# Output tiles treated four at a time, third products accumulated on their own, small filter operations on GpSimd, and a new order

## The chip, the cores and the metric

The kernel runs on one core of a Trainium2 chip. That core has five engines that work at the same time: TensorE (PE) for matmuls, VectorE (DVE) and GpSimd (POOL) for elementwise work, ScalarE (ACT) for activations, scalings and copies out of the matmul accumulators (PSUM), and SyncE (SP), whose queue issues most transfers. GpSimd's queue issues the transfers that add what they carry to what lies at their destination. The metric is the device time of one execution in microseconds; lower is better.

## The reference

The input x has 2,048 steps of 640 channels. Two branches are computed from it and mixed by a gate of one number per step:

```
g = sigmoid(sum(x * gate_w))                       # one gate per step
a = x * (irfft(rfft(kv) * rfft(ssm_k)) + kv * D)   # kv = (k filtered by 4 taps) * v; one filter of 2,048 taps per channel
h = shift(gelu(layernorm(x) @ w1)) @ w2            # four channel groups shifted by +1, -1, +2, -2 steps
x1 = x + h
b = x1 + gelu(layernorm(x1) @ w3) @ w4
out = g * a + (1 - g) * b
```

The four shifts of the hidden layer and the causal filter of 2,048 taps per channel are what make it more than a chain of matmuls.

## The kernel before

**The filter branch.** The 640 channels are five chunks of 128. The 2,048 steps are four blocks of 512. Each block is transformed by matmuls with the matrices of a folded real Fourier transform (`h_chunk` for the filter, `x_fwd` for kv); before that, `h_fold`, `h_even`, `kv` and `kv2` fold the data by its symmetries on DVE. The result of a chunk lies in `HF` (filter) and `XF` (signal): four blocks, a real and an imaginary part, 512 values. `unit(c)` then forms, for a chunk c, each output block o as the sum over a <= o of filter block a times signal block o - a. It treats output blocks in pairs: blocks 2 and 3 first, then 0 and 1. A complex product is made of three real ones: two in one instruction (into places 0 and 1 of an accumulator) and a third from the sum of real and imaginary part (place 2). For a > 0 the products go to a second buffer `TT`, and all three are added to the accumulator `ACC` in one instruction of DVE, or by one accumulating transfer of GpSimd's queue. Two subtractions and additions then write the block's real and imaginary part over `XF`.

**The end.** `final(g, o, q, k)` makes two tiles of 128 steps of output block o: tile 4o + q and its mirror 4o + 3 - q, for channel group g (g = 0 is chunks 0 to 2, 384 channels; g = 1 is chunks 3 and 4, 256 channels). PE computes the even and the odd half of the inverse transform, ACT copies them out, DVE forms their sum (first tile) and difference, PE turns the difference upside down with a flip matmul, ACT scales it by the gate, DVE multiplies by x. For g = 0 an accumulating transfer adds the pair to the output; for g = 1 DVE adds the other branch, which lies in `X`, and SP stores the result. There are 16 such calls. `base` and `mm4` write the other branch of the first 384 columns to the output: a store and an accumulating transfer for each tile. An accumulating transfer of `final` comes after those of the same tiles.

**The order.** Every instruction is recorded as an operation with what it reads and writes. `SEQUENCE` is a list of all 1,171 operations, written out; each engine and queue takes its own in that order and waits, by semaphores, for those of other engines that it depends on. `PLACES` puts the matmul results into PSUM banks. `ON` is a string of digits: wherever the program has a choice (`turn`: scale on ACT or DVE, copy by DVE or by transfer, add by DVE or by transfer), a 1 takes the other one than the default. `schedule` also keeps large transposing transfers and large accumulating transfers apart: each kind waits for the ones of the other kind that stand ahead of it in the list.

**GpSimd before.** Its queue has 44 operations: 15 small powers for the layer norms (`pool_pow`), 5 accumulating transfers of `unit`, 16 of `mm4` and 8 of `final`.

Of the kernel before, what the change touches and what calls it, by code (L numbers as in the profile page):

```python
# [446 lines left out]
def bass_gated_mix__ssm_conv_h3__mixer_s_mlp__prompt_kernel(  # L447
# [34 lines left out]
    def ps(n, cls):  # L482
# [3 lines left out]
    SEQUENCE = [1, 4, 5, 6, 26, 7, 3, 45, 24, 8, 0, 49, 50, 51, 55, 48, 68, 9, 10, 11, 12, 13, 14, 15, 16, 69, 17,  # L486
# [59 lines left out]
    PLACES = [4, 1, 7, 6, 5, 4, 6, 1, 1, 7, 0, 6, 3, 0, 2, 1, 3, 2, 3, 6, 7, 2, 1, 2, 7, 3, 5, 0, 3, 6, 4, 1, 1, 6,  # L546
# [622 lines left out]
```

## Time and profile before

| | us |
|---|---|
| median of 3 runs (221.81 to 223.04) | 221.84 |
| the profiled execution | 222.27 |
| its span, first to last instruction | 220.2 |
| VectorE busy | 212.1 |
| TensorE busy | 209.0 |
| ScalarE busy | 196.5 |
| GpSimd busy | 45.7 |

The span is what the trace covers; the profiled execution took 2.07 us more than that. Nearly all elementwise work of DVE is recorded under line 660 (`tt`), ACT's under line 670 (`act`), the matmuls under line 692 (`mm`), and transfers under line 237, because helpers record them. A group of instructions is therefore told apart by its shape. Records of consecutive instructions overlap a little, and ends of matmuls are modelled, so that busy time and count times mean differ.

### The profile page before, as it was taken

How to read it: one execution, taken by the hardware profiler on the slowest of the kernel's cores; microseconds unless marked ns; L12 is line 12 of the kernel's file. 1: busy time of each engine (PE TensorE's matmuls, PEld its weight loads, DVE VectorE, ACT ScalarE, POOL GpSimd, SP SyncE). 2: the span in 40 equal slices, each digit the busy share in tenths (PEclk: the TensorE clock that was granted, in tenths of full speed). 3: DMA queues.
4: the chain of work that ended last, by engine and by line, in shares of the span. 5: the costliest groups of instructions: out<-in, count | busy, mean ns of one | idle time of the engine just before them, and what ended most of it. 6: DMA issues, size and time to landing. Idle time of an engine off the chain costs nothing.

```text
span 220.2 us, 3837 instructions
## 1 busy us (share of the span) xinstructions
PE 209.0 (95%) x1401; PEld 125.7 (57%) x1410; DVE 212.1 (96%) x418; ACT 196.5 (89%) x326; POOL 45.7 (21%) x48
## 2 busy tenths in 40 slices
PE   6899999999999999999999999999999999999961
PEld 2598755554664446665446565456665445776730
DVE  5999999999999999999999999999999998999993
ACT  2499999999999999999999999999798978558981
POOL 1331102400010001001380103331101060645440
PEclk9999999999999999999999999999999999999995
DMA  6999998999979995898486893793198299366696
GB/s 170 346 233 214 246 207 231 177 236 193 284 246 204 383 198 95 162 174 185 120 147 110 201 193 43 163 174 71 19 160 182 65 219 246 39 74 71 74 179 119
DMA packets 79440, 37.73 MB, mean 171 GB/s; under 512 B 59001, under 2 KB 76990, under 8 KB 79422
## 3 DMA queue, kind: packets, MB, share of 16 engines
q1 hardware_dynamic: 73920, 31.91, 63.3%
q0 software_dynamic: 5328, 5.51, 18.9%
q8 instruction: 11, 0.18, 0.3%
q10 hardware_dynamic: 174, 0.07, 0.2%
q14 instruction: 7, 0.06, 0.1%
HBM read 14.88 MB, written 5.77 MB: 94 GB/s over the span
## 4 chain that ended last, share of the span: by engine, by line
DVE 57%; PE 28%; DMA 5%; ACT 5%; issue 3%; SPq 0%
DVE arena L660 46%; PE PSall L692 28%; ACT arena L670 5%; DVE arena L665 4%; DMA arena<-arena 3%; DVE arena L861 3%; DVE arena L980 2%; DMA arena<-in_A_q_dram 2%; DVE arena L946 1%; DVE arena L862 0%; DVE arena L866 0%; SPq L237 0%; DVE arena L735 0%; DVE arena L704 0%
## 5 line engine op out<-in xcount | busy, mean ns | idle before, releaser
L692 PE MATMUL PSall<-arena 128*128 128x512 bf16 (+5 forms) x1340 | 201.7, 309 | 3.4 <-ACT arena L670 1.3
L660 DVE TENSOR_TENSOR arena<-arena 128x1024 bf16<-128x1024 bf16 (+14 forms) x270 | 175.1, 712 | 1.7 <-DMA arena<-arena 0.9
L692 PEld LDWEIGHTS PSall<-arena 128*128 128x128 bf16 x1349 | 121.6, 98 | 82.7 <-ACT arena L670 3.3
L670 ACT ACTIVATE arena<-PSall 128x512 bf16<-128x512 f32 (+7 forms) x157 | 94.1, 659 | 9.6 <-PE PSall L750 4.9
L670 ACT ACTIVATE arena<-arena 128x640 bf16<-128x640 bf16 (+5 forms) x107 | 93.5, 904 | 1.9 <-DVE arena L660 1.8
L237 POOL DMA_DIRECT2D out_dram<-arena x24 | 24.1, 1133 | 67.7 <-ACT arena L670 51.7
L869 POOL TENSOR_TENSOR arena<-arena 128x2 f32<-128x2 f32 (+2 forms) x15 | 17.3, 1157 | 58.0 <-DVE arena L866 42.3
L670 ACT ACTIVATE arena<-PSall,arena 128x640 bf16<-128x640 f32 (+2 forms) x32 | 20.5, 652 | 6.8 <-PE PSall L692 6.6
L237 POOL DMA_DIRECT2D arena<-arena x5 | 4.9, 978 | 43.2 <-DVE arena L660 43.2
L980 DVE SCALAR_TENSOR_TENSOR arena<-PSall,arena 128x640 bf16<-128x640 f32 x16 | 12.9, 816 | 0.3
L665 DVE TENSOR_SCALAR arena<-arena 128x640 bf16<-128x640 bf16 (+6 forms) x35 | 11.9, 358 | 0.1
L861 DVE BATCH_NORM_STATS2 arena<-arena 128x6 f32<-128x320 bf16 x20 | 9.0, 484 | 1.3 <-DMA arena<-in_A_q_dram 1.3
L715 PE MATMUL PSall<-arena 128*128 128x512 bf16 x15 | 5.4, 529 | 2.2 <-DVE arena L712 2.2
L670 ACT ACTIVATION_READ_ACCUMULATOR arena<-arena 128x1 f32 x28 | 5.7, 204 | 0.0
L946 DVE TENSOR_SCALAR arena<-arena 32x256 bf16<-32x256 bf16 (+1 forms) x22 | 5.3, 240 | 0.4
L715 PEld LDWEIGHTS PSall<-arena 128*128 128x128 bf16 x15 | 1.8, 128 | 5.0 <-issue 2.5
L922 PE MATMUL PSall<-arena 128*128 128x128 bf16 x40 | 3.4, 220 | 0.9 <-DVE arena L665 0.9
L922 PEld LDWEIGHTS PSall<-arena 128*128 128x128 bf16 x40 | 2.4, 97 | 1.3 <-DVE arena L665 1.3
L866 DVE SCALAR_TENSOR_TENSOR arena<-arena 128x2 f32<-128x2 f32 (+2 forms) x19 | 2.9, 155 | 0.0
L718 ACT ACT_TABLE_LOAD x1 | 1.3, 1283 | 1.3 <-PEq L1154 1.3
L862 DVE BATCH_NORM_AGGREGATE arena<-arena 128x2 f32<-128x12 f32 x10 | 1.7, 192 | 0.0
L980 DVE DVE_READ_ACCUMULATOR arena<-PSall,arena 128x1 f32 x16 | 1.3, 80 | 0.0
(19 smaller groups left out, 2.9 us busy)
## 6 DMA issues: line engine op xcount, KB each, us to landing
arena<-in_A_ssm_k_dram SPq DMA_DIRECT2D x5, 512.0 KB, 5.2
arena<-in_A_q_dram SPq DMA_DIRECT2D x6, 320.0 KB, 5.7
arena<-in_B_w_dram SPq DMA_DIRECT2D x1, 1920.0 KB, 8.4
out_dram<-arena SPq DMA_DIRECT2D x16, 96.0 KB, 3.9
arena<-arena POOLq DMA_DIRECT2D x4, 384.0 KB, 5.0
out_dram<-arena POOLq DMA_DIRECT2D x16, 96.0 KB, 3.6
arena<-in_A_q_dram SPq DMA_DIRECT2D x8, 192.0 KB, 4.1
out_dram<-arena POOLq DMA_DIRECT2D x8, 192.0 KB, 4.0
```

The costliest lines, as they stand in the source:

```text
L237: fn = lambda e: e.dma_start(out, in_, **kw)
L660: P.op(eng, lambda e: e.tensor_tensor(o, real(a), real(b), op), [a, b], [o], dve_ns(o, [a, b], 2) if eng == "dve" else 500)
L665: P.op(eng, lambda e: e.tensor_scalar(o, real(a), s1, s2, op0=op0, **({} if op1 is None else {"op1": op1})), [a] + aps, [o], dve_ns(o, [a] ...
L670: P.op("act", lambda e: e.activation(real(o), real(a), f, bias=bias, scale=scale, **({"accum_out": accum} if accum is not None else {})), ...
L692: fns.append(lambda e, l=l, r=r, i=i: e.matmul(real(o), l, r, start=(i == 0), stop=(i == last)))
L715: P.op("pe", lambda e: e.matmul(real(pw), warm[:, 0:128], warm[:, 128:640], start=True, stop=True), [warm], [pw], 427.0 if i < 14 else 216.0)
L861: P.op("dve", lambda e, o=o, i=i: e.bn_stats(o, i), [i], [o], 400)
L866: P.op("dve", lambda e: e.scalar_tensor_tensor(o, a, x, b, op0=op0, op1=op1), [a, b] + aps, [o], n_of(o) / 0.96 + 65)
L869: P.op("pool", lambda g: g.tensor_tensor(o, a, e, ALU.pow), [a, e], [o], dur)
L922: P.op("pe", [lambda e, c=c, pb=pb, xn=xn: e.transpose(real(pb)[:, 128 * c:128 * (c + 1)], xn[:, 128 * c:128 * (c + 1)], ident) for c in r ...
L946: P.op("dve", lambda e, o=hT[q, 4, c0:c0 + n], i=hx[q, :]: e.tensor_scalar(o, i, 1.0, None, op0=ALU.mult), [hx[q, :]], [hT[q, 4, c0:c0 + n ...
L980: P.op("dve", lambda e: e.scalar_tensor_tensor(x, real(pr), 1.0, x, op0=ALU.mult, op1=ALU.add, accum_out=st[1, 0][:, t:t + 1]), [pr, x], [ ...
```

## The change

- `unit` adds the third product by itself where o0 = 2 and a is 1 or 2: the first two are added in one step, the third in another, each by DVE or by transfer according to `ON`, with a transfer as the third's default. `ACC` and `TT` are laid out with the three places outermost. From chunk 2 on, the third product for a = 2 has a buffer of its own, `TB2`. Chunk 4 is treated in three steps (blocks 2 and 3, then 1, then 0).
- `final(g, o, k)` makes all four tiles of an output block: one load of x, one sum and one difference for both halves, one product and one store or accumulating transfer for four tiles in their natural order. Only the last block of g = 1 is still treated tile by tile. There are 8 calls. The buffers `gyA` are three of four tiles (five of two before), `abA` two (four before).
- Small operations of `h_fold` and `h_even` (columns of 1 and 4 values, rows of 512 values on one partition) go to GpSimd unless `ON` keeps them on DVE.
- The DVE copy in `mm1` that moves shifted groups names the column before its own as read.
- `SEQUENCE` (now 1,147 operations), `PLACES` and `ON` are new throughout. With the new `ON`, three of the 25 small operations stay on DVE. `unit` has ten accumulating transfers: eight of a third product, one of the first two products, one of a whole sum. GpSimd's queue has 67 operations.

```diff
-    SEQUENCE = [1, 4, 5, 6, 26, 7, 3, 45, 24, 8, 0, 49, 50, 51, 55, 48, 68, 9, 10, 11, 12, 13, 14, 15, 16, 69, 17,
...
+    SEQUENCE = [26, 1, 8, 5, 0, 4, 6, 25, 3, 9, 10, 11, 12, 27, 13, 14, 15, 16, 28, 46, 52, 45, 39, 53, 49, 50, 54,
...
-    ACC, TT = [V(oB + 3072 * i, 3072).rearrange("p (o m n) -> p o m n", o=2, m=3) for i in range(2)]
+    ACC, TT = [V(oB + 3072 * i, 3072).rearrange("p (m o n) -> p m o n", m=3, o=2) for i in range(2)]
+    TB2 = V(oHF + 4096, 1024).rearrange("p (o n) -> p o n", o=2)
...
+    quad = lambda o, n: V(o, 4 * n).rearrange("p (t d) -> p t d", t=4)
+    qA = [quad(o, 384) for o in (oHF + 8192, oHF + 9728, oHF + 5120, oHF + 6656)]
+    qB = [quad(oHF + 12288 + 1024 * k, 256) for k in range(4)]
+    abA = [quad(oW2 + 1536 * i, 384) for i in range(2)]
+    gyA = [quad(o, 384) for o in (oHF, oHF + 1536, oB + 12288)]
+    abB = [quad(oB + 8192 + 1024 * i, 256) for i in range(4)]
+    gyB = [quad(oHF + 16384 + 1024 * i, 256) for i in range(4)]
...
+    def small_tt(o, a, b, op):
+        tt(o, a, b, op, "dve" if turn(False) else "pool")
...
-        tt(k[:, 0, 0:1], k[:, 0, 0:1], Dcol[:, c:c + 1], ALU.add)
+        small_tt(k[:, 0, 0:1], k[:, 0, 0:1], Dcol[:, c:c + 1], ALU.add)
...
-            tt(fo[:, e, :, 128], k[:, :, 384], k[:, :, 128], op)
+            small_tt(fo[:, e, :, 128], k[:, :, 384], k[:, :, 128], op)
...
-        tt(o[0:1, 0, 0], ev[0:1, 1, :, 0], ev[0:1, 0, :, 0], ALU.add)
-        tt(o[0:1, 1, 0], ev[0:1, 1, :, 0], ev[0:1, 0, :, 0], ALU.subtract)
+        small_tt(o[0:1, 0, 0], ev[0:1, 1, :, 0], ev[0:1, 0, :, 0], ALU.add)
+        small_tt(o[0:1, 1, 0], ev[0:1, 1, :, 0], ev[0:1, 0, :, 0], ALU.subtract)
...
-                         [hx[q, :]], [hT[q, 4, c0:c0 + n]], n / 3.84 + 65)
+                         [hx[q, :], hT[q, 4, c0 - 1:c0]], [hT[q, 4, c0:c0 + n]], n / 3.84 + 65)
...
-    ADDS = ()
+    SPLIT = ((2, 1), (2, 2))
...
-        for o0 in (2, 0):
-            for a in range(o0 + 2):
+        for o0, o1 in ((2, 4), (0, 2)) if c < 4 else ((2, 4), (1, 2), (0, 1)):
+            for a in range(o1):
...
+                own = a == 2 and c >= 2
...
+                third = TB2[:, 0:n] if own else to[:, 2]
...
-                if turn((o0, a) in ADDS):
-                    P.dma("pool", acc, tmp, accum=True)
-                else:
-                    tt(acc, acc, tmp, ALU.add)
+                parts = [(acc[:, 0:2], tmp[:, 0:2], False), (acc[:, 2], third, True)] if (o0, a) in SPLIT else [(acc, tmp, False)]
+                for x, y, away in parts:
+                    if turn(away):
+                        P.dma("pool", x, y, accum=True)
+                    else:
+                        tt(x, x, y, ALU.add)
...
+    def final(g, o, k):
...
+        qt, gy, ab = (qA, qB)[g][k], (gyA[k % 3], gyB[k])[g], (abA[k % 2], abB[k])[g].rearrange("p (q e) d -> p q e d", q=2)
+        rows = lambda a, t, m: bass.AP(a.tensor, a.offset + 128 * (4 * o + t) * D + 128 * c0, [[D, 128], [128 * D, m], [1, n]])
+        P.dma(sp, qt, rows(A_q, 0, 4))
+        for q in range(2):
+            scale(qt[:, q], qt[:, q], gst[3][:, 4 * o + q:4 * o + q + 1], True)
+        last = g == 1 and o == 0
+        both = [slice(q, q + 1) for q in range(2)] if last else [slice(0, 2)]
+        for q in range(2):
+            pr = ps(2, "inv")[:, :, 0:n]
...
+            act(ab[:, q], pr, ACTF.Copy)
+        for h in both:
+            tt(gy[:, h], ab[:, h, 0], ab[:, h, 1], ALU.add)
+            tt(ab[:, h, 1], ab[:, h, 0], ab[:, h, 1], ALU.subtract)
+        for q in range(2):
+            pf = ps(1, "fl")[:, 0:n]
+            mm(pf, [(flip, ab[:, q, 1])])
+            act(gy[:, 3 - q], pf, ACTF.Copy, scale=gst[3][:, 4 * o + 3 - q:4 * o + 4 - q])
+        for h in [slice(t, t + 1) for t in (0, 3, 1, 2)] if last else [slice(0, 4)]:
             tt(gy[:, h], gy[:, h], qt[:, h], ALU.mult)
+            if g:
+                tt(gy[:, h], gy[:, h], X[:, 4 * o + h.start:4 * o + h.stop, hs], ALU.add)
+                P.dma(sp, rows(out, h.start, h.stop - h.start), gy[:, h])
+            else:
+                P.dma("pool", rows(out, 0, 4), gy, accum=True)
...
         for o in (3, 2, 1, 0):
-            for q in range(2):
-                at(final, g, o, q, 2 * (3 - o) + q)
+            at(final, g, o, 3 - o)
```

More of the change, by code (lines that the diff above doesn't have):

```diff
@@ L484, in ps @@
         return v if n == 1 else v.rearrange("p (b n) -> p b n", b=2)
-    SEQUENCE = [1, 4, 5, 6, 26, 7, 3, 45, 24, 8, 0, 49, 50, 51, 55, 48, 68, 9, 10, 11, 12, 13, 14, 15, 16, 69, 17,
[59 rows of a table removed]
-    PLACES = [4, 1, 7, 6, 5, 4, 6, 1, 1, 7, 0, 6, 3, 0, 2, 1, 3, 2, 3, 6, 7, 2, 1, 2, 7, 3, 5, 0, 3, 6, 4, 1, 1, 6,
[6 rows of a table removed]
-    ON = ("0000000011111111011011111111111100010000010000101111000000000000001000010010000100000100000100000000"
-          "0000000000000000000000000000000")
+    SEQUENCE = [26, 1, 8, 5, 0, 4, 6, 25, 3, 9, 10, 11, 12, 27, 13, 14, 15, 16, 28, 46, 52, 45, 39, 53, 49, 50, 54,
[57 rows of a table added]
+    PLACES = [6, 3, 4, 7, 4, 6, 2, 4, 7, 3, 4, 3, 0, 1, 6, 0, 1, 2, 0, 2, 6, 1, 1, 7, 5, 4, 5, 1, 2, 7, 3, 2, 7, 6,
[6 rows of a table added]
+    ON = ("0000000011111111111111111111000000111000000011101000000000000000001011110000100000000100000100100000"
+          "1010000010000100100000000000000100000001001000000000000000000000000")
     HW = S + 4
@@ L613, in bass_gated_mix__ssm_conv_h3__mixer_s_mlp__prompt_kernel @@
     pair = lambda o, n: V(o, 2 * n).rearrange("p (t d) -> p t d", t=2)
-    qA = [pair(oHF + 8192 + 768 * k if k < 5 else oHF + 4096 + 768 * (k - 5), 384) for k in range(8)]
-    qB = [pair(oHF + 12288 + 512 * k, 256) for k in range(8)]
-    abA = [pair(oW2 + 768 * i, 384) for i in range(4)]
-    gyA = [pair(oHF + 768 * i, 384) for i in range(5)]
-    abB = [pair(oB + 8192 + 512 * i, 256) for i in range(8)]
-    gyB = [pair(oHF + 16384 + 512 * i, 256) for i in range(8)]
+    quad = lambda o, n: V(o, 4 * n).rearrange("p (t d) -> p t d", t=4)
[5 more added lines that the diff above has]
+    gyB = [quad(oHF + 16384 + 1024 * i, 256) for i in range(4)]
     sm = V32(oSm, 388)
@@ L862, in ln_bn, with stt @@
         P.op("dve", lambda e: e.bn_aggr(bna[:, t, :], bns[k]), [bns[k]], [bna[:, t, :]], 120)
-    def stt(o, a, x, b, op0, op1):
+    def stt(o, a, x, b, op0, op1, eng="dve"):
         aps = [x] if not isinstance(x, float) else []
-        P.op("dve", lambda e: e.scalar_tensor_tensor(o, a, x, b, op0=op0, op1=op1), [a, b] + aps, [o], n_of(o) / 0.96 + 65)
+        P.op(eng, lambda e: e.scalar_tensor_tensor(o, a, x, b, op0=op0, op1=op1), [a, b] + aps, [o], n_of(o) / 0.96 + 65)
     def pool_pow(o, a, e, dur=900):
@@ L1021, in unit @@
         tt(H4[:, :, 1], H4[:, :, 1], H4[:, :, 0], ALU.subtract)
-        for o0 in (2, 0):
-            for a in range(o0 + 2):
+        for o0, o1 in ((2, 4), (0, 2)) if c < 4 else ((2, 4), (1, 2), (0, 1)):
+            for a in range(o1):
                 lo = max(o0, a)
-                n, x0 = o0 + 2 - lo, lo - a
-                acc, tmp = ACC[:, lo - o0:2], TT[:, 0:n]
+                n, x0 = o1 - lo, lo - a
+                own = a == 2 and c >= 2
+                acc, tmp = ACC[:, :, lo - o0:o1 - o0], TT[:, :, 0:n]
                 to = tmp if a else acc
+                third = TB2[:, 0:n] if own else to[:, 2]
                 u, v = H4[:, a, 1], HD[:, a]
                 uv = bass.AP(u.tensor, u.offset, [u.ap[0], [0, n], [v.offset - u.offset, 2], [1, 512]])
-                tt(to[:, :, 0:2], X4[:, x0:x0 + n], uv, ALU.mult)
-                tt(to[:, :, 2], SX[:, x0:x0 + n], H4[:, a, 0].unsqueeze(1).to_broadcast([128, n, 512]), ALU.mult)
+                tt(to[:, 0:2].rearrange("p m o n -> p o m n"), X4[:, x0:x0 + n], uv, ALU.mult)
+                tt(third, SX[:, x0:x0 + n], H4[:, a, 0].unsqueeze(1).to_broadcast([128, n, 512]), ALU.mult)
                 if not a:
                     continue
-                if turn((o0, a) in ADDS):
-                    P.dma("pool", acc, tmp, accum=True)
-                else:
-                    tt(acc, acc, tmp, ALU.add)
-            Y = XF[:, c, o0:o0 + 2]
-            tt(Y[:, :, 0], ACC[:, :, 2], ACC[:, :, 1], ALU.subtract)
-            tt(Y[:, :, 1], ACC[:, :, 2], ACC[:, :, 0], ALU.add)
-            scale(Y[0:1, :, :, 0:128], ACC[0:1, :, 0:2, 0:128], 1.0, True)
-    def final(g, o, q, k):
+                parts = [(acc[:, 0:2], tmp[:, 0:2], False), (acc[:, 2], third, True)] if (o0, a) in SPLIT else [(acc, tmp, False)]
[4 more added lines that the diff above has]
+                        tt(x, x, y, ALU.add)
+            Y, R = XF[:, c, o0:o1], ACC[:, :, 0:o1 - o0]
+            tt(Y[:, :, 0], R[:, 2], R[:, 1], ALU.subtract)
+            tt(Y[:, :, 1], R[:, 2], R[:, 0], ALU.add)
+            scale(Y[0:1, :, :, 0:128].rearrange("p o r n -> p r o n"), R[0:1, 0:2, :, 0:128], 1.0, True)
+    def final(g, o, k):
         c0, c1 = GROUPS[g]
@@ L1046, in final @@
         hs = slice(128 * c0, 128 * c1)
-        ta, tb = 4 * o + q, 4 * o + 3 - q
-        qt, gy, ab = (qA, qB)[g][k], (gyA[k % 5], gyB[k])[g], (abA[k % 4], abB[k])[g]
-        two = lambda a: a[:, ta:tb + 1:tb - ta, hs]
-        rows = lambda a, lo, m: bass.AP(a.tensor, a.offset + 128 * ta * D + lo, [[D, 128], [128 * D * (tb - ta), 2], [1, m]])
-        P.dma(sp, qt, rows(A_q, 128 * c0, n))
-        scale(qt[:, 0], qt[:, 0], gst[3][:, ta:ta + 1], True)
-        pr = ps(2, "inv")[:, :, 0:n]
-        for e in range(2):
-            mm(pr[:, e].rearrange("p (c d) -> p c d", d=128), [(G[:, j, e ^ (j // 2), 128 * q:128 * (q + 1)], XF[:, c0:c1, o, e ^ (j // 2), 128 * j:128 * (j + 1)])
-                          for j in range(4)])
@@ L1057, in final @@
-        act(ab, pr, ACTF.Copy)
-        tt(gy[:, 0], ab[:, 0], ab[:, 1], ALU.add)
-        tt(ab[:, 1], ab[:, 0], ab[:, 1], ALU.subtract)
-        pf = ps(1, "fl")[:, 0:n]
-        mm(pf, [(flip, ab[:, 1])])
-        act(gy[:, 1], pf, ACTF.Copy, scale=gst[3][:, tb:tb + 1])
-        if not g:
-            tt(gy, gy, qt, ALU.mult)
-            P.dma("pool", rows(out, 0, n), gy, accum=True)
-            return
-        for h in (slice(0, 2),) if k < 6 else (slice(0, 1), slice(1, 2)):
-            tt(gy[:, h], gy[:, h], qt[:, h], ALU.mult)
-            tt(gy[:, h], gy[:, h], two(X)[:, h], ALU.add)
-            t = ta if h.start == 0 else tb
-            P.dma(sp, bass.AP(out.tensor, out.offset + 128 * t * D + 128 * c0, [[D, 128], [128 * D * (tb - ta), h.stop - h.start], [1, n]]), gy[:, h])
+        qt, gy, ab = (qA, qB)[g][k], (gyA[k % 3], gyB[k])[g], (abA[k % 2], abB[k])[g].rearrange("p (q e) d -> p q e d", q=2)
@@ new lines, in final @@
+        rows = lambda a, t, m: bass.AP(a.tensor, a.offset + 128 * (4 * o + t) * D + 128 * c0, [[D, 128], [128 * D, m], [1, n]])
[6 more added lines that the diff above has]
+            pr = ps(2, "inv")[:, :, 0:n]
+            for e in range(2):
+                mm(pr[:, e].rearrange("p (c d) -> p c d", d=128), [(G[:, j, e ^ (j // 2), 128 * q:128 * (q + 1)], XF[:, c0:c1, o, e ^ (j // 2), 128 * j:128 * (j + 1)])
+                              for j in range(4)])
+            act(ab[:, q], pr, ACTF.Copy)
```

128 rows, old and new, of tables (PLACES, SEQUENCE) are left out of this document.

## The prediction

> **What bounds the kernel now.** I read the totals first, then busy time by stretch, then the chain of waits, then the groups by shape. The first line is the engines' totals; the next three are stretches (start:end, then busy us of each engine, instruction counts in brackets).
>
> ```profile
> PE 209.0 (95%) x1401; PEld 125.7 (57%) x1410; DVE 212.1 (96%) x418; ACT 196.5 (89%) x326; POOL 45.7 (21%) x48
> 10.00:199.00 189.00, 188.10 (x1259) 112.91 (x1265) 186.77 (x335) 178.01 (x290) 36.10 (x34) 1.00 0.84 174
> 199.00:209.00 10.00, 9.59 (x75) 7.04 (x74) 9.93 (x26) 9.67 (x20) 4.50 (x4) 1.00 0.67 73
> 209.00:217.00 8.00, 4.30 (x28) 2.32 (x26) 7.84 (x29) 5.62 (x12) 2.38 (x2) 0.82 0.92 156
> ```
>
> From 10 to 199 us TensorE and VectorE are both full: 0.9 us of recorded idle on PE, 2.2 us on DVE. After 199 DVE stays full (17.77 of 18 us) and PE empties. So the run has a body in which two engines run abreast, and a tail of 18 us in which DVE is the bound. The chain and PE's timeline say the same (start us, length us, what):
>
> ```profile
> 176.97 6.79 DMA arena<-arena
> 205.95 4.19 DVE arena L660 x16
> 210.19 5.25 DVE arena L660 x18
> 216.66 0.29 DVE arena L660
> 213.31 0.28 PE L692 MATMUL PSall<-arena 128*128 128x256 bf16 x1 [1.16 <-ACT arena L670]
> 214.82 0.61 PE L692 MATMUL PSall<-arena 128*128 128x256 bf16 x2 [0.49 <-DVE arena L660]
> L692 PE MATMUL PSall<-arena 128*128 128x512 bf16 x48 | 10.5, 379 | 0.0
> ```
>
> DVE ends at 216.95 us and the span at 220.2, so 3.25 us follow it. One accumulating transfer (176.97) holds DVE up. The last row is PE between 100 and 110 us: 48 matmuls of 512 columns in 10 us, one each 0.21 us, with no idle time. The change leaves the matmuls as they are. Hence what it takes from DVE in the body can bring PE's stream forward only by what PE loses there now.
>
> **DVE's work, recounted.** Durations by shape (count | busy us of the group, mean ns of one):
>
> ```profile
> L660 DVE TENSOR_TENSOR arena<-arena 128x1024 bf16<-128x1024 bf16 (+14 forms) x270 | 175.1, 712 | 1.7 <-DMA arena<-arena 0.9
> L660 DVE TENSOR_TENSOR arena<-arena 128x3072 bf16<-128x3072 bf16 x9 | 15.7, 1749 | 0.1
> L660 DVE TENSOR_TENSOR arena<-arena 128x2048 bf16<-128x2048 bf16 x40 | 48.1, 1214 | 0.1
> L660 DVE TENSOR_TENSOR arena<-arena 128x1536 bf16<-128x1536 bf16 x16 | 15.1, 947 | 0.2 <-ACT arena L670 0.2
> L660 DVE TENSOR_TENSOR arena<-arena 128x1024 bf16<-128x1024 bf16 x80 | 52.0, 682 | 1.0 <-DMA arena<-arena 0.9
> L660 DVE TENSOR_TENSOR arena<-arena 128x768 bf16<-128x768 bf16 x8 | 4.4, 550 | 0.0
> L660 DVE TENSOR_TENSOR arena<-arena 128x512 bf16<-128x512 bf16 x22 | 9.0, 417 | 0.1
> L660 DVE TENSOR_TENSOR arena<-arena 128x384 bf16<-128x384 bf16 x16 | 5.4, 348 | 0.0
> L660 DVE TENSOR_TENSOR arena<-arena 128x256 bf16<-128x256 bf16 x24 | 6.1, 283 | 0.1
> L660 DVE TENSOR_TENSOR arena<-arena 1x512 bf16<-1x512 bf16 x10 | 4.1, 408 | 0.0
> L660 DVE TENSOR_TENSOR arena<-arena 128x4 bf16<-128x4 bf16 x10 | 1.6, 166 | 0.0
> L665 DVE TENSOR_SCALAR arena<-arena 128x2048 bf16<-128x2048 bf16 x4 | 2.9, 733 | 0.0
> L665 DVE TENSOR_SCALAR arena<-arena 128x640 bf16<-128x640 bf16 x16 | 6.6, 430 | 0.0
> ```
>
> By the first row 270 instructions of 0.712 us (192.2) keep DVE busy for 175.1 us, so each runs 0.063 us into the next, and an instruction saved is worth its duration less 0.063.
>
> - Small filter operations. The choices (the n-th digit of ON flips the n-th choice) send 22 to GpSimd: ten of 1x512, nine of 128x4, three of 128x1 (taken as 0.15). 4.08 + 1.49 + 0.45 - 22 x 0.063 = 4.6 us off DVE.
> - Adds in unit. Before, 9 of 3,072 and 6 of 1,536 elements; after, 9 of 2,048, 2 of 1,024 and 9 of 1,536, the rest going by ten transfers instead of five: 21.4 - 20.8 + 5 x 0.063 = 0.9 us off. That is little: the thirds leave, but transfers that carried whole adds come back.
> - Finals. Before: 16 each of 384 and 256, 8 of 768, 12 of 512, 8 of 256, in all 21.8 us in 60 instructions. After: 8 of 768, 6 of 512, 4 of 256, 4 of 1,536, 6 of 1,024, 8 of 256, in all 18.2 us in 36. 3.6 - 24 x 0.063 = 2.1 us off.
> - Unit 4 in three steps instead of two: four instructions more, 0.4 us on.
> - Choices that swap DVE and ACT: a tap of 2,048 and a normalisation of 640 come to DVE (0.73, 0.43), with six short copies (an estimate of 0.25 each, below the 0.43 of 640 elements), and one near 0.4 leaves: 2.25 less seven overlaps, 1.8 us on.
>
> Sum: 4.6 + 0.9 + 2.1 - 0.4 - 1.8 = 5.4 us off DVE, of 212.1. At most 2.1 of it lies in the tail.
>
> **What it is worth in the body.** PE's columns do not change, so I take only the 0.9 us that PE idles there by record; the bounds are 3 us sooner, were more of PE's loss hidden in the modelled ends, and 2 us later, if the new order stalls it somewhere. Two new costs lie here.
>
> First, accumulating transfers.
>
> ```profile
> arena<-arena POOLq DMA_DIRECT2D x4, 384.0 KB, 5.0
> arena<-arena POOLq DMA_DIRECT2D x1, 768.0 KB, 6.5
> out_dram<-arena POOLq DMA_DIRECT2D x16, 96.0 KB, 3.6
> out_dram<-arena POOLq DMA_DIRECT2D x8, 192.0 KB, 4.0
> out_dram<-arena SPq DMA_DIRECT2D x4, 64.0 KB, 2.0
> out_dram<-arena SPq DMA_DIRECT2D x6, 128.0 KB, 2.5
> ```
>
> Eight of the new ten carry 256 KB, so about 4.5 us each. I added up DVE's work from each product to the first instruction that needs the sum or overwrites the source. Unit 0's transfer has 6.3 us and unit 1's last one 5.1; in units 3 and 4 two follow one another, with 10.4 us for the pair, just enough. If one lands like that of 176.97 (6.79 us) DVE waits some 2 us. DVE's 5.4 us of relief covers that, so I cost it at nothing; without that cover it is 2 to 4 us. Behind a waiting transfer the GpSimd queue holds the small operations and normalisation powers that follow it; their readers on PE come some 8 us of PE work later.
>
> Second, GpSimd beside DVE.
>
> ```profile
> L869 POOL TENSOR_TENSOR arena<-arena x15: 560/858/3991, 4.5 to 142.6; 128x2 f32<-128x2 f32 x8, 128x1 f32<-128x1 f32 x4, 128x4 f32<-128x4 f32 x3
> 109.89 3.99 POOL L869 TENSOR_TENSOR arena<-arena 128x4 f32<-128x4 f32 x1
> 109.44 5.02 DVE L660 TENSOR_TENSOR arena<-arena 128x1024 bf16<-128x1024 bf16 x6
> ```
>
> One GpSimd power took 3.99 us beside six DVE instructions that ran their normal time (two of 1,024, three of about 2,048 and one of 1x512: 5.4 less five overlaps of 0.063 is 5.1; 5.02 measured). So GpSimd waited and DVE did not. But those powers read four numbers at most, and the new ones read 512. I take no cost to DVE, by that row; the bounds are 0 and 10 x 1.16 us (the 15 powers' 17.3 us over 15, if each instruction shut DVE out for its whole length).
> [...]
>
> **Start and tail.**
>
> ```profile
> 3.09 1.04 SPq L237 DMA_DIRECT2D arena<-in_B_w_dram  x2
> 9.08 0.82 PE L692 MATMUL PSall<-arena 128*128 128x128 bf16 x15
> 200.74 0.91 POOL L237 DMA_DIRECT2D out_dram<-arena  x1 [1.78 <-ACT arena L670]
> L670 ACT ACTIVATE arena<-PSall 128x768 bf16<-128x768 f32 x3 | 2.4, 792 | 0.1
> L670 ACT ACTIVATE arena<-PSall 128x512 bf16<-128x512 f32 x8 | 4.7, 588 | 0.1
> L670 ACT ACTIVATE arena<-PSall,arena 128x384 bf16<-128x384 f32 x4 | 2.3, 578 | 0.4 <-PE PSall L692 0.4
> L670 ACT ACTIVATE arena<-PSall,arena 128x256 bf16<-128x256 f32 x8 | 3.7, 473 | 1.0 <-PE PSall L692 1.0
> ```
>
> The last four rows are ACT's after 199.2 us. PE's first real matmul is at 9.08 us, and needs half of w1. The half that is used first is now issued one place sooner on SP (two issues take 1.04 us, so 0.5 us sooner), but the first tile is normalised behind more statistics. I take 0.3 us sooner, from 0 to 0.5.
>
> The last MLP tile has left ACT when its transfer is issued, at 200.74. From there the new order gives ACT one inverse of 768, four of 512 and two of 768, three flips of 384 and four of 256, two scalings and two short row copies (the last four at an estimated 0.45) before the inverses of final g = 0, o = 0 are all evicted: 2.4 + 2.4 + 1.7 + 1.9 + 1.8, less 1.0 for overlaps like DVE's, is 9.2 us, so about 209.7. That final's buffer is also gyA[0], which final g = 0, o = 3 used: its 384 KB transfer waits for the MLP tile's (3.6 us, 204.3) and takes about 5, to 209.3. Both say 209 to 209.7; I take 209.2. DVE then has 20 instructions: two of 768, twelve of 256, three of 1,024, one of 1,536 and two of 512, 8.3 less 20 x 0.063 = 7.1 us, to 216.3 where it was 216.95. But the last store is now 256 KB instead of 64: by the rows of 64 and 128 KB (0.5 us per 64 KB) 1.5 more, by those of 384 and 768 KB 0.75; I take 0.9. Tail: -0.65 + 0.9 = +0.25, from -1.5 to +1.5. So most of what DVE saves at the end goes into coarser steps.
>
> The profiled execution took 222.27 us, 2.07 over its span and 0.43 over the median. Its change is -0.3 - 0.9 + 0.25 = -0.95; taken off the median, 221.84, that is 220.9.
>
> **Rivals.** About 1% is what can be told from no change here.
> - As worked out: 220.9, its own range 219.6 to 222.5. For it: PE full in the body. Chance 0.45 with the rest of the cases within 1%.
> - The relief reaches PE: the new order has no stall in the body (-3.0), and tail and start give -0.3 between them: 218.5, its own range 217.3 to 219.6. For it: 5.4 us of slack that DVE never had, and ACT 11 us short of full in the body. Against it: 0.9 us of recorded idle. Chance 0.30.
> - GpSimd shuts DVE out: each of the ten 1x512 operations stops DVE for 0.56 us (the shortest power) to 1.16. That is 5.6 to 11.6 us against 5.4 saved, and the tail's +0.25: 222.3 to 228.3, about 225.3. It eats the saving from 0.54 us each, and passes 1% slower from about 0.75 each. For it: the 3.99 us show the two engines do meet at something. Against it: no DVE instruction was stretched. Chance 0.20.
> - The accumulation does not leave DVE: two of the ten thirds stay (units 0 and 2), and the waits on paired transfers come at 2 to 4 us uncovered: 224.5. Chance 0.05.
>
> Faster 0.30, same 0.45, slower 0.25. The range is 217.8 to 225.5: it leaves out the fastest quarter of the fast case (0.07) and the upper half of the third (0.10).
>
> **What would show it.** DVE busy near 206.7 with the 2,048 group at 1,214 ns: the recount holds. Any DVE group longer than before, or DVE idle released by nothing, next to GpSimd rows of 1x512: the third case. PE full from 10 to 199 with no earlier end: the body as worked out. DVE waiting at final g = 0, o = 0 near 209 on a GpSimd transfer or on ACT, and a last store of 3 us: the tail. A last matmul before 212 us would prove me wrong on the fast side.

## The result and the profile after

The changed kernel takes 236.27 us (median of 4 runs, 234.85 to 236.62) against 221.82 us before (median of 4): a ratio of 1.063, with a 95% interval from 1.057 to 1.068. It is 6% slower, outside my range and past its slow end. The profiled execution took 234.85 us, with a span of 233.1.

Totals of the changed kernel:

```profile
PE 211.6 (91%) x1401; PEld 125.2 (54%) x1410; DVE 216.8 (93%) x388; ACT 194.4 (83%) x323; POOL 77.0 (33%) x71
```

DVE has 30 instructions fewer than before and is busy 4.7 us longer. GpSimd has 23 more and is busy 31 us longer. Busy time by stretch of the changed kernel (start:end, length, then PE, PEld, DVE, ACT and POOL with instruction counts, the granted clock, the DMA share and GB/s):

```profile
10.00:199.00 189.00, 178.40 (x1157) 103.84 (x1163) 179.13 (x304) 168.54 (x274) 64.00 (x53) 0.98 0.81 170
95.00:103.00 8.00, 1.23 (x9) 0.66 (x8) 7.96 (x10) 2.07 (x6) 7.39 (x1) 0.74 0.43 88
103.00:110.00 7.00, 7.00 (x37) 3.83 (x36) 3.93 (x7) 5.21 (x7) 1.42 (x1) 0.80 1.09 158
102.53:105.70 3.17, 3.17 (x9) 1.29 (x10) 0.61 (x2) 1.27 (x2) 0.00 (x0) 0.50 0.73 135
```

The second and third stretch of the kernel before, for comparison:

```profile
95.00:103.00 8.00, 8.00 (x48) 4.50 (x46) 8.00 (x10) 8.00 (x11) 0.14 (x1) 1.00 1.16 183
103.00:110.00 7.00, 7.00 (x34) 3.19 (x33) 7.00 (x11) 6.89 (x9) 2.46 (x4) 1.00 0.50 124
```

In eight microseconds PE has 9 matmuls where it had 48. When it starts again, at 102.53, after 6.77 us without a matmul, it works for 3.2 us at a granted clock of 0.50 (the fourth line), and from 105.70 to 110 us at 1.00; the kernel before has 1.00 over both stretches. That makes the mean of 0.80 over the third stretch and costs some 1.6 us more, an estimate: half of those 3.2 us.

The chain of waits of the changed kernel leads to the cause (start us, length us, what):

```profile
73.23 8.83 DMA arena<-in_A_ssm_k_dram
82.06 0.08 issue
82.14 20.26 POOL arena L660 x5
102.40 0.14 issue
102.53 11.37 PE PSall L695 x54
```

Five small operations on GpSimd take 20 us, and PE waits for the last. (The first of them waits for a filter transfer that takes 8.83 us. The run e8 below leaves that transfer as it is and removes PE's wait, so the transfer is not the cause.) The timelines of GpSimd, DVE and PE in that stretch show them singly (idle time before, and its releaser, in brackets):

```profile
84.74 5.19 POOL L660 TENSOR_TENSOR arena<-arena 128x1 bf16<-128x1 bf16 x1
91.10 11.28 POOL L660 TENSOR_TENSOR arena<-arena 1x512 bf16<-1x512 bf16 x1
89.80 1.39 DVE L665 TENSOR_SCALAR arena<-arena 128x384 bf16<-128x384 bf16 x2
91.08 10.30 DVE L660 TENSOR_TENSOR arena<-arena 128x1024 bf16<-128x1024 bf16 x13
101.42 1.12 DVE L665 TENSOR_SCALAR arena<-arena 1x512 bf16<-1x512 bf16 x1
102.53 7.68 PE L695 MATMUL PSall<-arena 128*128 128x512 bf16 x37 [6.77 <-POOL arena L660]
```

The 11.28 us are one row of 512 values (`h_even`, chunk 2). It starts 0.02 us after the first of 13 two-input additions and products of DVE. These run without a break, each in its normal time, until 101.38. DVE then pauses for 0.04 us. The row is done about 1 us later, and the DVE instruction that began there took 1.12 us instead of 0.34 (the mean of the same shape in a kernel below). The addition of one column (128x1) had lasted 5.19 us beside eight two-input instructions. It ended at 89.93 without a gap of DVE, just after the first of the two one-input instructions of 89.80 had begun; the second of those took 1.16 us, beside the next GpSimd row. So GpSimd was shut out here while DVE ran such two-input instructions on end (5.19 us beside eight, 11.28 beside 13), and where it got in, one DVE instruction was longer (1.12 us instead of 0.34).

The second half of that can be read in DVE's groups. First the changed kernel, then one described below that has the rows on DVE (e6; count | busy us, mean ns of one):

```profile
L949 DVE TENSOR_SCALAR arena<-arena 32x512 bf16<-32x512 bf16 x8 | 3.2, 406 | 0.1
L869 DVE SCALAR_TENSOR_TENSOR arena<-arena 128x4 f32<-128x4 f32 x9 | 2.4, 265 | 3.4 <-ACT arena L670 3.4
L665 DVE TENSOR_SCALAR arena<-arena 128x8 bf16<-128x8 bf16 x5 | 1.9, 381 | 0.0
```

```profile
L948 DVE TENSOR_SCALAR arena<-arena 32x512 bf16<-32x512 bf16 x8 | 2.3, 286 | 0.1
L868 DVE SCALAR_TENSOR_TENSOR arena<-arena 128x4 f32<-128x4 f32 x9 | 1.4, 152 | 0.0
L664 DVE TENSOR_SCALAR arena<-arena 128x8 bf16<-128x8 bf16 x5 | 0.9, 181 | 0.0
```

Nine DVE instructions beside GpSimd's are 0.4 to 1.0 us longer than the shortest of their kind, 7.2 us in all; in e6 none is. Only three of the nine follow a recorded gap of DVE (0.01, 0.04 and 0.03 us). The other six begin 0.08 us before the instruction ahead of them ends, as neighbours on a full DVE do. Two of these six come after an instruction with an input in PSUM, the other four are short one-input instructions (32x512, 128x8) and operations on two or four values.

### The profile page after: what moved, and what is told of

Same layout as the page of the kernel before. It is cut to its first block, busy times and chain, and to the rows that moved or that the text cites. A ratio compares the mean times of both kernels' runs of the same rounds, so it can differ in the third digit from the quotient of the medians.

```text
span 233.1 us, 3829 instructions
## 1 busy us (share of the span) xinstructions
PE 211.6 (91%) x1401; PEld 125.2 (54%) x1410; DVE 216.8 (93%) x388; ACT 194.4 (83%) x323; POOL 77.0 (33%) x71
## 4 chain that ended last, share of the span: by engine, by line
DVE 49%; PE 16%; DMA 10%; ACT 10%; POOL 9%; issue 3%; SPq 0%; DVEq 0%; POOLq 0%
DVE arena L660 41%; PE PSall L695 13%; ACT arena L670 10%; POOL arena L660 9%; DMA arena<-arena 6%; DMA arena<-in_A_ssm_k_dram 4%; DVE arena L665 2%; PE PSall L718 2%; DVE arena L983 2%; DVE arena L949 2%; DVE arena L869 1%; SPq L237 0%; PE PSall L925 0%; DVEq L1146 0%; DVE arena L715 0%
## 5 line engine op out<-in xcount | busy, mean ns | idle before, releaser
L695 PE MATMUL PSall<-arena 128*128 128x512 bf16 (+5 forms) x1340 | 204.3, 310 | 14.1 <-POOL arena L660 6.8
L660 DVE TENSOR_TENSOR arena<-arena 128x1024 bf16<-128x1024 bf16 (+10 forms) x233 | 172.9, 798 | 6.2 <-ACT arena L670 3.6
L670 ACT ACTIVATE arena<-arena 128x640 bf16<-128x640 bf16 (+7 forms) x103 | 89.7, 897 | 8.4 <-DVE arena L660 7.4
L660 POOL TENSOR_TENSOR arena<-arena 1x512 bf16<-1x512 bf16 (+2 forms) x22 | 35.0, 1612 | 26.7 <-DMA arena<-in_A_ssm_k_dram 17.3
L872 POOL TENSOR_TENSOR arena<-arena 128x2 f32<-128x2 f32 (+2 forms) x15 | 15.2, 1016 | 43.0 <-DVE arena L869 29.4
L237 POOL DMA_DIRECT2D out_dram<-arena x20 | 21.1, 1495 | 23.1 <-DVE arena L660 11.0
L237 POOL DMA_DIRECT2D arena<-arena x10 | 9.4, 937 | 57.0 <-DVE arena L660 40.1
L665 DVE TENSOR_SCALAR arena<-arena 128x640 bf16<-128x640 bf16 (+7 forms) x40 | 15.7, 412 | 0.2
L869 DVE SCALAR_TENSOR_TENSOR arena<-arena 128x2 f32<-128x2 f32 (+2 forms) x19 | 4.9, 260 | 3.4 <-ACT arena L670 3.4
L949 DVE TENSOR_SCALAR arena<-arena 32x256 bf16<-32x256 bf16 (+1 forms) x24 | 6.8, 282 | 0.7 <-ACT arena L670 0.3
```

Of the source, the lines that this page charges most:

```text
L237: fn = lambda e: e.dma_start(out, in_, **kw)
L660: P.op(eng, lambda e: e.tensor_tensor(o, real(a), real(b), op), [a, b], [o], dve_ns(o, [a, b], 2) if eng == "dve" else 500)
L665: P.op(eng, lambda e: e.tensor_scalar(o, real(a), s1, s2, op0=op0, **({} if op1 is None else {"op1": op1})), [a] + aps, [o], dve_ns(o, [a] ...
L670: P.op("act", lambda e: e.activation(real(o), real(a), f, bias=bias, scale=scale, **({"accum_out": accum} if accum is not None else {})), ...
L695: fns.append(lambda e, l=l, r=r, i=i: e.matmul(real(o), l, r, start=(i == 0), stop=(i == last)))
L869: P.op(eng, lambda e: e.scalar_tensor_tensor(o, a, x, b, op0=op0, op1=op1), [a, b] + aps, [o], n_of(o) / 0.96 + 65)
```

## The experiments

I had three theories. **One**: GpSimd is shut out while DVE runs two-input instructions back to back, and PE waits for what it makes. **Two**: the new order itself is late, whoever does the small operations. **Three**, for what is left: the accumulating transfers are not hidden. ON is written below by choice number, counted from 0.

**All 22 small operations back on DVE** (e1), and **only the two rows of chunk 2** (e2), in the changed kernel:

```diff
-    ON[51:53] = "00"     # h_even(2): even0, even1 on GpSimd
+    ON[51:53] = "11"     # e2: on DVE; e1: the other 20 choices as well
```

> The changed kernel with all 22 small filter operations back on DVE; the order and everything else as in the changed kernel. Theory 1 (GpSimd is shut out while DVE runs two-input instructions back to back, and PE waits for its row): the 6.8 us wait of PE at 95.8 and the 1.6 us of low clock behind it go, GpSimd no longer stretches DVE, DVE gets 4.6 us of small operations back but loses some 7 us of stretching; about 226 us (225 to 228.5). Theory 2 (the new order itself is late in the middle, whoever does the rows): PE still waits at the same matmul, 232 to 237 us.

> The changed kernel with only the two row operations of h_even for chunk 2 back on DVE; twenty small operations stay on GpSimd. Theory 1: the one long wait (11.3 us for one row of 512) is what costs, so this alone gives nearly all of it, 8.4 us less: about 227.8 us (226.5 to 229.5), and the stretched DVE instructions elsewhere stay. If the cost were spread over all the small operations (each stretching DVE by about 0.9 us), this gives a tenth to a fifth of what all 22 give: about 234 us. Theory 2: no gain, 235 to 237 us.

Measured: 227.62 us for e1 (1.025 of the kernel before, 1.021 to 1.028) and 229.36 for e2 (1.035, 1.031 to 1.038). Two rows of 22 operations give 6.9 of the 8.65 us, and theory two as the main cause falls: the order is the same in all three. In e1 PE is full in the stretch where it had stood:

```profile
95.00:103.00 8.00, 8.00 (x57) 5.39 (x55) 8.00 (x10) 7.95 (x14) 0.00 (x0) 1.00 1.01 197
```

**The same 22 operations on GpSimd in the kernel before** (e3), with its own order:

```diff
+    def small_tt(o, a, b, op, stay=False):
+        tt(o, a, b, op, "dve" if stay else "pool")
...
-        tt(o[0:1, 0, 0], ev[0:1, 1, :, 0], ev[0:1, 0, :, 0], ALU.add)
+        small_tt(o[0:1, 0, 0], ev[0:1, 1, :, 0], ev[0:1, 0, :, 0], ALU.add)
...
```

> The kernel before, in its own order, with the same 22 small operations on GpSimd and nothing else changed. Theory 1: DVE runs back to back here as well, so GpSimd is shut out somewhere, some rows last 4 us or more, and PE waits for one: 4 to 12 us slower than the kernel before, 226 to 234 us. Theory 2 (only the new order is at fault): 4.6 us come off DVE, and the time stays or falls, 219 to 222 us.

Measured: 229.35 us, a ratio of 1.033 (1.030 to 1.037). Taking 22 instructions off the busiest engine makes the kernel before 7.4 us slower. Its GpSimd timeline has the same sight, two rows in 10.58 us. The other two lines are from its chain and from DVE's timeline:

```profile
152.67 10.58 POOL L660 TENSOR_TENSOR arena<-arena 1x512 bf16<-1x512 bf16 x2 [2.00 <-DVE arena L660]
163.20 3.70 DMA arena<-arena
166.93 2.43 DVE L660 TENSOR_TENSOR arena<-arena 128x1024 bf16<-128x1024 bf16 x3 [1.26 <-DMA arena<-arena]
```

The loss takes another way here than I expected: PE waits for a GpSimd row once, for 1.8 us. The two rows hold up the accumulating transfer behind them on GpSimd's queue, DVE waits for that transfer, ACT waits for DVE, and PE waits 2.0 us for ACT. Besides, DVE is busy 216.3 us with 22 instructions fewer, against 212.1: eight DVE instructions are 7.4 us longer in all than the shortest of their kind, more than the 4.6 us that I had counted off DVE for these operations.

**The contention by itself** (e4), in a program of its own:

```diff
+    def stage(n, make, after=1):          # n DVE instructions of 128x1024
+        for i in range(n):
...
+            make(i, here)
+            if i == after:                # then four rows of 1x512 on GpSimd
+                for j in range(4):
...
+                    row(o, here[0:1, 0:512], src2[0:1, 0:512])
```

> Not the computation: the output is filled with zeros, and six trains of 12 or 16 DVE instructions of 128x1024 run, each with four GpSimd row additions of 1x512 released after the second DVE instruction. Theory 1: a row alone takes about 1.1 us. Beside two-input instructions back to back the first row waits for the end of the train (16 x 0.62, some 8 us) and DVE is not stretched. Beside one-input instructions rows and DVE run undisturbed, or alternate. With a one-input instruction every fourth place, or with each instruction waiting for the one before, a row gets in at such a place, and the DVE instruction after it is stretched by about 0.9 us. With one input from PSUM no conflict. If GpSimd were only slow and not shut out, rows take the same 1.1 to 1.5 us in all the trains.

Measured: the first GpSimd row of each train in its timeline. In order: alone; beside 16 two-input instructions; beside 12 of one input; two inputs with every fourth of one input; two inputs, each waiting for the one before; one input from PSUM (128x512); two f32 inputs (128x512). The last line is DVE's instruction beside the fifth.

```profile
3.96 1.14 POOL L421 TENSOR_TENSOR arena<-arena 1x512 bf16<-1x512 bf16 x1 [3.52 <-DVE arena L412]
10.15 9.36 POOL L421 TENSOR_TENSOR arena<-arena 1x512 bf16<-1x512 bf16 x1 [1.73 <-DVE arena L412]
24.02 4.28 POOL L421 TENSOR_TENSOR arena<-arena 1x512 bf16<-1x512 bf16 x1 [1.20 <-DVE arena L415]
33.35 8.29 POOL L421 TENSOR_TENSOR arena<-arena 1x512 bf16<-1x512 bf16 x1 [1.73 <-DVE arena L412]
46.82 1.65 POOL L421 TENSOR_TENSOR arena<-arena 1x512 bf16<-1x512 bf16 x1 [1.86 <-DVE arena L412]
58.92 1.14 POOL L421 TENSOR_TENSOR arena<-arena 1x512 bf16<-1x512 bf16 x1 [5.79 <-DVE arena L418]
66.44 6.95 POOL L421 TENSOR_TENSOR arena<-arena 1x512 bf16<-1x512 bf16 x1 [3.05 <-DVE arena L412]
47.50 1.52 DVE L412 TENSOR_TENSOR arena<-arena 128x1024 bf16<-128x1024 bf16 x1
```

Alone a row takes 1.14 us. Beside an unbroken train with both inputs in SBUF it waits for the train's end, 9.36 us with 16 instructions, and no DVE instruction is stretched (the 16 and a row ahead of them take 10.05 us). Where each DVE instruction waits for the one before (a gap of 0.03 us), GpSimd gets in at once, and the DVE instruction that follows takes 1.52 us instead of 0.69. With an input in PSUM the row takes 1.14 us, as alone, and DVE's 12 instructions take 7.25 us without a break. Two of my expectations missed: one-input instructions on bf16 shut GpSimd out just as well, alone (4.28 us) or mixed in (8.29 us). In these trains it is the gap that lets it in, not the one input. In the kernels a gap is not the only way in. Six of the nine places above have none: in the changed kernel an operation on four values that begins, at 122.29, 0.08 us before its two-input predecessor (128x2046) ends takes 1.12 us instead of 0.15, beside a row of 1.23 us. What lets GpSimd in there is not settled by these runs.

**A wait added on DVE** (e8), with all 22 operations left on GpSimd:

```diff
+    for i, before in ((653, 649), (654, 653), (388, 654)):   # DVE instructions in the run of 13
+        P.ops[i].preds.setdefault(before, False)
     P.alts = alts
```

> The changed kernel, all 22 small operations on GpSimd as there, with three waits ADDED on DVE: in the run of two-input instructions that shut the row out from 91.1 to 101.4 us, three consecutive instructions of unit 0 and chunk 1 each wait for the one before (a gap of 0.03 us). If GpSimd gets in at any such gap: the row of 11.3 us takes 1.2 to 2 us, one DVE instruction is 0.85 us longer, PE's wait of 6.8 us goes, and the added waits make the kernel 7 to 8.5 us faster: about 228 us (227 to 229.5). If the row is slow for another reason (its data, its queue), nothing changes: 235 to 237 us.

Measured: 230.69 us (1.039, 1.035 to 1.042), 5.6 us faster than the changed kernel for three added waits, less than the 7 to 8.5 expected. The row that took 11.28 us takes 1.67, and PE is full from 87.8 to 112.2 us. A little later another GpSimd operation takes 5.43 us, a power of the layer norms, which took 1.42 us in the changed kernel:

```profile
92.31 1.67 POOL L660 TENSOR_TENSOR arena<-arena 1x512 bf16<-1x512 bf16 x1
104.87 5.43 POOL L872 TENSOR_TENSOR arena<-arena 128x4 f32<-128x4 f32 x1 [10.89 <-DVE arena L869]
```

**What is left.** e1 is still 5.6 us above the kernel before. Its longest stall of DVE in the first 40 us is this (DVE's timeline):

```profile
27.41 0.25 DVE L659 TENSOR_TENSOR arena<-arena 128x1 bf16<-128x1 bf16 x2 [1.83 <-DMA arena<-in_A_ssm_k_dram]
```

DVE's queue stands behind a filter that has not landed. Three kernels follow: the mixed one (e5) leaves the six column operations of chunks 0 and 1 on GpSimd; the second (e6) also stops keeping 256 KB accumulating transfers apart from large transposing ones; the third (e7) is e5 with unit 3's thirds on DVE.

```diff
+    ON[28:31] = "000"; ON[38:41] = "000"    # e5, e6, e7: GpSimd, the other 16 on DVE
-            elif o.eng == "pool" and o.nbytes > 200000:
+            elif o.eng == "pool" and o.nbytes > 300000:    # e6
-    ON[119] = ON[121] = "0"
+    ON[119] = ON[121] = "1"                 # e7
```

> The changed kernel with 16 of the 22 small operations on DVE, and the six column operations of chunks 0 and 1 (1 or 4 values each, before 31 us) left on GpSimd. With all 22 on DVE the first addition of chunk 1 held DVE's queue for 1.83 us until its filter had landed, and PE fell 3.4 us back between 22 and 34 us, which the changed kernel did not. If that is what putting them back costs, most of the 3.4 us come back: 224.3 us (223.3 to 226). If the early delay is of another kind, 226.5 to 228.

> The mixed kernel (six small operations on GpSimd), and the accumulating transfers of 256 KB are no longer kept apart from the large transposing ones. In the changed kernel the chain of waits runs from 169.4 to 185.4 us through one transposing and two accumulating transfers of unit 3 in a row (5.95, 5.15, 3.74 us), with 1.3 us of waiting on DVE at its end. If keeping them apart costs time, 1 to 2 us less than the mixed kernel: about 223 us. If the accumulating transfers are hidden anyway, as I predicted, the same within 0.5 us; if the two kinds slow one another, up to 2 us more.

> The mixed kernel with unit 3's two third products added by DVE instead of by transfers. DVE gets 2 x 0.62 us of work and loses the 1.1 to 1.3 us of waiting for the second transfer. If the two transfers were hidden, 1.2 us slower than the mixed kernel; if their wait is on the path, the same within 0.4 us, or faster where the next transfers on GpSimd's queue come sooner.

Measured: 225.52 us (1.015, 1.012 to 1.019), 224.25 (1.010, 1.007 to 1.013) and 225.64 (1.016, 1.013 to 1.020). So putting the early column operations back on DVE had cost 2.1 us, somewhat less than I expected. Keeping the transfers apart costs some 1.3 us, though the intervals of e5 and e6 just touch. And doing unit 3's thirds on DVE costs nothing, so their transfers had saved nothing. The chain of the changed kernel shows why; the first transfer is the transposing one, the others are unit 3's two thirds:

```profile
169.41 5.95 DMA arena<-arena
175.36 0.02 issue
175.40 0.52 issue
175.92 5.15 DMA arena<-arena
181.06 0.02 issue
181.10 0.51 issue
181.61 3.74 DMA arena<-arena
```

Each waits for the one before, and 1.3 us of it reach DVE.

**More off DVE** (e9), on top of e6:

```diff
-    ON[85] = "1"; ON[76] = "1"; ON[139] = "1"
+    ON[85] = "0"     # unit 0, a = 1: third by transfer
+    ON[76] = "0"     # a normalisation back on ACT
+    ON[139] = "0"    # a scaling back on ACT
```

> The mixed kernel without the keeping apart of large transfers, and three more choices turned to take work off DVE: the third product of unit 0 for a = 1 goes by a transfer (0.62 us), and one normalisation of 640 and one scaling of 384 go back to ACT (0.43 and 0.31 us, less their overlaps). If DVE is what sets the time from there to the end, 1.0 us less than without them: about 223.2 us. If PE or ACT is, the same as without them, 224.2 us, or up to 0.5 us more.

Measured: 226.97 us (1.023, 1.019 to 1.028), 2.7 us slower than e6, against all three cases. In its chain the one new transfer takes 8.07 us, where the median of 256 KB is 3.6:

```profile
72.90 8.07 DMA arena<-arena
```

DVE waits 2.08 us for it, and PE 2.4 us for DVE. Whether the busy DMA engines (a share of 0.94 from 60 to 80 us) or GpSimd beside DVE make it so long was not tested, nor were the three edits tried one by one.

**The kernel before, with the two edits that helped**: without the keeping apart (e11), and also with the six early column operations on GpSimd (e10).

```diff
-            elif o.eng == "pool" and o.nbytes > 200000:
+            elif o.eng == "pool" and o.nbytes > 800000:    # both
-        tt(k[:, 0, 0:1], k[:, 0, 0:1], Dcol[:, c:c + 1], ALU.add)
+        small_tt(k[:, 0, 0:1], k[:, 0, 0:1], Dcol[:, c:c + 1], ALU.add, c < 2)    # e10, and fold128 likewise
```

> The kernel before, its accumulating transfers of 384 and 768 KB no longer kept apart from the large transposing ones, and nothing else changed. Its only wait of DVE after the start is 0.89 us at 183.8, for a transfer that had itself waited. If that is a loss that the keeping apart makes, 0.5 to 1 us faster: 221.0 us. If not, no change, or up to 1 us slower where the two kinds slow one another.

> As the kernel before without the keeping apart, and besides the six column operations of chunks 0 and 1 (1 or 4 values) on GpSimd, where the mixed kernel has them. They take 0.6 us off DVE before 35 us; there PE is full in the kernel before, so if PE sets the pace of the body, no further gain: within 0.3 us of the kernel before without the keeping apart. If GpSimd is shut out by DVE here too, 1 us slower or more.

Measured: 221.90 us (0.998, 0.996 to 1.000) and 221.18 us (0.995, 0.993 to 0.997). The first is no change that can be told. The second is 0.5% faster than the kernel before and the fastest of all; it is 0.7 us below e11, with intervals that just overlap, where I expected at most 0.3. Why was not followed up.

## Why the prediction was wrong

**The step that failed** is "GpSimd beside DVE", with its "I take no cost to DVE, by that row", and the sentence ahead of it that small operations may be late because "their readers on PE come some 8 us of PE work later". The row (a power of 3.99 us beside six DVE instructions in their normal time) said in so many words that GpSimd waits. I asked only what that costs DVE, and put GpSimd's own wait at nothing. But 3.99 us is no bound. There GpSimd got in before DVE paused: the power ended at 113.88, the six instructions at 114.46. Beside the 13 two-input instructions it did not get in until they had ended. The wait was 11.28 us for one row and 20 us for five operations, more than the 8 us of cover. Of the 14.4 us, 10.7 go with the 16 operations that e5 has back on DVE, 1.3 with the keeping apart of transfers (e6), and some 2 stay.

**The third rival** had the right place and half of the mechanism: GpSimd shuts DVE out. That half measured 7.2 us over nine DVE instructions, within its 5.6 to 11.6. The other half, PE's 6.8 us wait and the estimated 1.6 us of half clock, it did not have, and so even its far end (228.3) was short. Its "from 0.54 us each" has no meaning where the loss comes from one operation: two rows of 22 operations gave 6.9 of 8.65 us. What GpSimd does while DVE's instructions follow one another without a gap I did not ask: here it waited out 13 of them (11.28 us).

**DVE's recount** (5.4 us off) held in its direction and not in its size. Added up over DVE's records of each profile, without the 16 that only read out an accumulator:

| | before | changed | e6 |
|---|---|---|---|
| sum of durations, us | 239.1 | 240.2 | 237.6 |
| overlap with the next, us (pairs) | 27.1 (344) | 23.5 (288) | 24.6 (308) |
| gaps below 0.15 us (count) | 1.6 (52) | 2.4 (73) | 2.2 (71) |
| longer gaps, us | 2.5 | 9.6 | 2.6 |
| end of DVE, us | 216.95 | 229.56 | 218.72 |

The changed kernel's durations without the 7.2 us of stretching are 233.0, so 6.1 less than before. But 56 overlapping pairs are gone (3.6 us), not the 30 that I took off at 0.063 us. Some 20 more instructions wait for something just before them, and such a one starts 0.03 us after its predecessor instead of 0.08 inside it. So 2.5 us came off DVE's busy time, not 5.4. In e6, where no row is on GpSimd, durations are 1.5 us less and overlaps and small gaps take 3.1 back; DVE ends 1.8 us later than before. By this account that is most of the 2 us by which e6 stays behind; no run tests it by itself.

**The body**: "PE's columns do not change", 0.9 us sooner with bounds of -3 and +2, was wrong in the upper bound: it allowed for a stall from the new order, and none for an operand that comes from GpSimd. Whether relief of DVE alone would have brought PE anything is not shown, since every run that takes work off DVE gives some to GpSimd, to its queue or to ACT.

**Accumulating transfers** "at nothing": not hidden, as the 1.3 us of e6 against e5 and the nil of e7 show. I had bounded an uncovered one at 2 to 4 us; what I left out of the sum is that two thirds in a row queue behind a transposing transfer as well.

**The start**: the first real matmul came at 8.57 us instead of 9.08, so 0.5 us sooner, the end of my 0 to 0.5:

```profile
8.57 0.84 PE PSall L695 x15
```

**The tail**: in e6 DVE's end is 3.6 us before the span's, where it was 3.25. The larger last store costs 0.33, not 0.9. DVE does not wait for a GpSimd transfer at the last final of g = 0, and for ACT only twice, for 0.2 us each, so the gate that I worked out at 209.2 did not bind.

## What to carry to other kernels

An instruction moved to GpSimd beside a full DVE had no duration of its own here: a row that takes 1.14 us alone took 11.28 beside a run of 13 two-input DVE instructions, and the DVE instruction behind them then took 1.12 us instead of 0.34. So ask of each one what DVE runs at that time, who needs the result and what stands behind it on GpSimd's queue, and put there only what can wait. The six column operations of e10, before 31 us, did no harm there (221.18 us against 221.90 in e11). A change that takes work off a full engine can still lengthen its run: e6 has 1.5 us less of DVE durations than the kernel before, and DVE ends 1.8 us later. By the account above most of that is overlap between neighbours (0.08 us a pair) that new waits (gaps of 0.03 us) take away; no run tests it by itself.

## What was not expected of the hardware

- Unbroken runs of two-input DVE instructions shut GpSimd out to their end (9.36 us beside 16 instructions, 11.28 us beside 13 in the kernel), and a gap of 0.03 us (e4) or 0.04 us (the changed kernel) let one GpSimd instruction in. It is not the only way in: six of nine stretched DVE instructions of the changed kernel have no gap before them. Three waits added on DVE made the kernel 5.6 us faster.
- One-input bf16 instructions of 128x1024 shut GpSimd out as two-input ones did (4.28 us beside the rest of 12); those of 128x512 with an input in PSUM did not (1.14 us, as alone).
- An accumulating transfer of 256 KB took 8.07 us at one place and 3.6 us in the median.
